# A spare PSUM bank as two halves in turn, in a planned attention and MLP kernel

## The chip, the cores and the metric

The kernel runs on one core of a Trainium2 chip. The metric is the device time of one execution in microseconds (us). "Span" is the time from the first to the last instruction of the profiled execution; it is about 1.8 us shorter than the device time of the same execution.

## The reference, cut to what matters

Two transformer layers with the same weights: layernorm, attention with 16 heads of 28 columns over 2048 tokens of 448 columns, then layernorm and an MLP of 1792 hidden columns with a squared ReLU.

```python
x = A_x
for layer in range(2):                      # the same weights twice
    h = layernorm(x)
    q, k, v = heads(h @ wqkv)               # 16 heads of 28
    p = softmax(q @ k.T * 28 ** -0.5)       # 16 x 2048 x 2048
    x = x + merge(p @ v) @ wo
    h = layernorm(x)
    x = x + relu(h @ w1 + b1) ** 2 @ w2 + b2
```

## The kernel before

The exponentials of the softmax are the largest single piece of work: 16 x 2048 x 2048 of them per layer, for both layers together done by ScalarE in 683 instructions ("exps" below) of 128 x 1536. Everything else is laid around them. A small planner inside the program does that before anything runs: each piece of work is an `Op` with an engine, an assumed duration, what it depends on and the buffer that it takes. The planner repeatedly issues the candidate that can start first by its own model. The order that comes out is fixed; on the chip each engine works its queue strictly in that order, and if the model was wrong, it stands.

```python
class Res:                                   # a buffer with n places
    def when(self):                          # when the next taker may have it
        k = len(self.rel)
        return 0.0 if k < self.n else self.rel[k - self.n]
...
    # in the planner: work of lower rank goes to TensorE only if it ends
    # no later than SLACK after the next exp's scores are due
    ok = [c for c in cands if c[2] != "PE" or c[1] == 0 or c[0] + c[3][2].dur <= due + SLACK]
    cands = ok or cands
```

The kernel uses eight PSUM banks. Six hold two score groups (three units of 512 columns each), one holds the value sums, and one spare bank takes everything else: projections, transposes, both MLP layers and the "fillers", matmuls without a use of their own that are meant to keep TensorE's clock up. (In the trace of this kernel the granted clock is 0.5 from 151.6 to 155.0 us, just after TensorE has stood for 3.06 us.) Emptying the spare bank into SBUF is called an eviction.

```python
R_sc, R_o, R_m, R_pt = Res(2), Res(1), Res(1), Res(4)
...
def bank(o, name):
    if o.res is R_m:
        return ps_m.tile([P, 512], DT.float32, name=name, tag="m")[:, :]
    return ps_sc.tile([P, 3 * 512], DT.float32, name="sc", tag="sc")[:, 0:512]
...
def mm_tile(subs, evac, ev_dur, deps, any_engine=False, sets=(), early=False):
    ...                                      # the matmuls of one tile into bank(first)
    e = Op(..., ev_dur, lambda e: evac(e, box["t"]), deps=[last], rel=first, sets=sets)
    yield e                                  # the eviction, in the same stream
    return e
```

A unit is one head's scores of one key block (128 keys) against 512 queries; three units make a group with one exp. `AHEAD = range(2)` tells how many of the four head groups of the second layer's second query block are begun before the last key blocks are needed. `SLACK = 0.7` is the microseconds by which lower work may overrun the time when the next scores are due.

```python
add_passes(1, [0], [0, 12])                  # layer 2, query block 0: keys 0..11
add_passes(1, [1], [0, 12], AHEAD)           # query block 1, some head groups: keys 0..11
add_passes(1, [0], [12, 16])                 # only now keys 12..15
```

The softmax denominators of most query blocks are spread over partitions through DRAM and broadcast back, by three queued transfers with assumed latencies:

```python
d1 = Op("DMA", 0.1, spread, deps=[oe])       # + 2.0 for any DMA
...
d2 = Op("DMA", 0.1, away, deps=[r1])
...
r = own = Op("DMA", 1.0, back, deps=[d2], acq=R_rec)
```

The softmax here doesn't subtract the row's maximum and nothing guards it: scores larger than these inputs give would overflow.

Of the kernel before, what the change touches and what calls it, by code (L numbers as in the profile page):

```python
# [23 lines left out]
AHEAD = range(2)  # L24
SLACK = 0.7
# [15 lines left out]
class Op:  # L41
    __slots__ = ("eng", "dur", "fn", "deps", "acq", "rel", "mode", "sets", "start", "end", "res", "turn", "ready")

    def __init__(self, eng, dur, fn, deps=(), acq=None, rel=None, mode="full", sets=()):
        self.eng = eng if isinstance(eng, tuple) else (eng,)
        self.dur, self.fn, self.deps, self.rel, self.mode = dur, fn, deps, rel, mode
        self.acq = acq if isinstance(acq, tuple) else (() if acq is None else (acq,))
        self.sets = sets if isinstance(sets, list) else ([sets] if sets else [])
        self.start = self.end = self.res = self.turn = None

# [4 lines left out]
class Planner:  # L55
# [3 lines left out]
    def __init__(self):  # L59
# [4 lines left out]
        self.past = []  # L64

# [5 lines left out]
    def spawn(self, prio, gen):  # L71
        self.streams.append([prio, gen, next(gen, None)])
        self.streams.sort(key=lambda s: s[0])

    def earliest(self, o):
        t = 0.0
        for d in o.deps:
# [5 lines left out]
            t = max(t, d.end + ((0.06 if same else 0.10) if d.eng[0] == "DVE" else  # L83
                                (0.0 if same and d.eng[0] != "DMA" else LAT[d.eng[0]])))
        if o.acq:
# [3 lines left out]
            t = max(t, min(free))  # L89
        o.ready = t  # L90
# [9 lines left out]
    def run(self):  # L100
        while self.streams:
# [20 lines left out]
            o.start, o.end = s, s + o.dur  # L122
            self.clock[e] = o.end
# [8 lines left out]
            st[2] = next(st[1], None)  # L132
# [5 lines left out]
def kernel(  # L138
# [40 lines left out]
    R_sc, R_o, R_m, R_pt = Res(2), Res(1), Res(1), Res(4)  # L179
    R_xt, R_os, R_xn, R_h, R_on, R_rec = Res(3), Res(2), Res(2), Res(1), Res(2), Res(2)  # L180
# [104 lines left out]
    def bank(o, name):  # L285

        if o.res is R_m:
            return ps_m.tile([P, 512], DT.float32, name=name, tag="m")[:, :]
# [11 lines left out]
    def layernorm(t0, nt, deps_of, early=False):  # L300
# [39 lines left out]
        def turn(p0, own, xs):  # L340
            def tr(e, xs=xs):
                tp = bank(t, "tp").bitcast(DT.bfloat16).rearrange("p (c q) -> p c q", c=NDC)
# [5 lines left out]
            t = Op("PE", 0.07 * NDC * len(xs), tr, deps=[x[1] for x in xs], acq=pools_now(early))  # L348
            yield t

            def ev(e, tp=box["t"], p0=p0, w=len(xs) * P):
# [6 lines left out]
            yield o  # L358
# [3 lines left out]
        for p0 in range(0, nt, 2):  # L362
            js = range(p0, min(p0 + 2, nt))
            own = Op("DVE", 0.0, None, acq=R_xn)
            yield own
            xs = []
            for j in js:
                xn = xns[2 * (own.turn % 2) + j % 2]
# [10 lines left out]
            if early and p0 + 2 < nt:  # L379
                continue  # L380
# [5 lines left out]
    def mm_tile(subs, evac, ev_dur, deps, any_engine=False, sets=(), early=False):  # L386
# [7 lines left out]
        while i < len(mms):  # L394
# [5 lines left out]
            def fn(e, part=mms[i:k], i=i):  # L400
                if i == 0:
                    box["t"] = bank(first, "mt")
                for c0, n, lhsT, rhs, a, b in part:
                    nc.tensor.matmul(box["t"][:, c0:c0 + n], lhsT=lhsT, rhs=rhs, start=a, stop=b)  # L404
            last = Op("PE", dur, fn, deps=list(deps) if i == 0 else [last],
                      acq=pools_now(early) if i == 0 else None)
# [3 lines left out]
        e = Op(engs_now(early) if any_engine else ("DVE",), ev_dur, lambda e: evac(e, box["t"]), deps=[last], rel=first, sets=sets)  # L410
        yield e
        return e

    def copy_to(dst):
        def f(e, t):
            src = t[:, :] if len(dst.shape) == 2 else t[:, :].rearrange("p (r n) -> p r n", r=dst.shape[1])
# [6 lines left out]
    def qkv(l, t0, nt, xnT, own_xt, ends, early=False):  # L423
        n, q0 = nt * P, t0 * P
        r = QB // n
        last = None

        def turned(w, dst, key, wkey, g0):
            nonlocal last
            d = dst[:, g0, q0:q0 + n] if r == 1 else dst[:, g0:g0 + r, q0:q0 + n]  # L430
            last = yield from mm_tile(
                [(i * n, n, [(w[:, dc, 4 * g:4 * g + 4, :], xnT[:, dc, 0:n]) for dc in range(NDC)])
                 for i, g in enumerate(range(g0, g0 + r))],
                copy_to(d), 0.70, [*ends, *[(wkey, g) for g in range(g0, g0 + r)]], True,
                [(key, l, g, tb) for g in range(g0, g0 + r) for tb in range(t0, t0 + nt)], early)

        def values():
            nonlocal last
            for tb in range(t0, t0 + nt):
                def evv(e, t, tb=tb):  # L440
                    o = V_sb[l][:, tb, :, 0:DH]
                    i = t[:, 0:D].rearrange("p (h r) -> p h r", r=DH)
                    if e == "ACT":
                        nc.scalar.copy(out=o, in_=i)
                    else:
                        nc.vector.tensor_copy(out=o, in_=i)  # L446
                j = tb - t0
                last = yield from mm_tile(
                    [(0, D, [(xnT[:, dc, j * P:(j + 1) * P], wv[:, dc, :]) for dc in range(NDC)])],
                    evv, 0.62, [*ends, ("wv",), *([("s", 1)] if early else [])], True, ("V", l, tb), early)  # L450

        ks = [(wk, K_sb[l], "K", "wk", g) for g in range(0, G, r)]
        qs = [(wq, Q_sb, "Q", "wq", g) for g in range(0, G, r)]
# [99 lines left out]
    def p_stream():  # L553
        for gi, us in enumerate(groups):
# [5 lines left out]
            for ri, run in enumerate(runs):  # L560
# [8 lines left out]
                def fn(e, gi=gi, us=us, run=run, box=box, opens=opens, l=l, g=g, kbs=kbs, r=r, n=n):  # L569
                    if opens:  # L570
                        box["t"] = ps_o.tile([P, QB], DT.float32, name="oT")
                    for i in range(r):
# [9 lines left out]
                       deps=[("e", gi), *{("V", l, us[k][1] + i) for k in run for i in range(r)}],  # L582
# [24 lines left out]
    def norm_stream(l, qb, g, res, oe):  # L607
# [6 lines left out]
        if tail:  # L614
            def den(e):
                box["t"] = bank(d, "den")
# [173 lines left out]
```

## Time and profile before

| kernel before | value | from |
|---|---|---|
| device time | 991.0 us median (987.35 to 991.94, 4 runs) | the runs beside the changed kernel |
| span, granted clock | 990.1 us, 0.990 | the profile by core |
| ScalarE / TensorE / VectorE busy | 937.5 / 913.4 / 419.5 us | the page, first part |
| first exp starts; tail after the last exp | 14.6; 31.5 us | the trace |
| typical distance of two exp starts | 1.33 us | the trace |
| gaps: all distances of exp starts, less 1.335 each | 32.4 us | the trace |
| of it short gaps (distance 1.375 to 2.6 us) | 25.8 us in 83 | the trace |
| of it long gaps (distance over 2.6 us) | 7.4 us in 2 | the trace |

This is one time budget: head, 682 distances of 1.335, gaps, last exp, tail. As long as the pace of 1.33 us stays, a change of the kernel shows in the head, the gaps and the tail and nowhere else. A gap that is named by its place ("after exp 351") is given as the whole distance of two exp starts. I use the split into short and long gaps. (Distances below 1.375 are in the total only, so the two kinds don't add up to it exactly.) The lines of the page and of the timeline are shown and read in the prediction. One more, of the groups by form: the eviction of the MLP's first layer, a whole bank, 691 ns each.

```profile
L701 DVE TENSOR_SCALAR r<-mt 128x512 bf16<-128x512 f32 x100 | 69.1, 691 | 89.6 <-PE mt L404 89.5
```

### The profile page before, as it was taken

To read this page: it belongs to the slowest core of one execution; us is meant where nothing else is said; L and a number is where in the kernel's file an instruction comes from. 1 tells how busy PE (TensorE), PEld (TensorE's weight loads), DVE (VectorE), ACT (ScalarE), POOL (GpSimd) and SP (SyncE) were. 2 spreads that over 40 slices of the span, in tenths; PEclk is the share of its full clock that TensorE was granted. 3 is DMA by queue.
4 is the path that set the end of the run, shared out by engine and by line. 5 is a ranking of instruction groups with operands and counts; after the bars stand their busy time and mean duration, and the time that the engine had idled before them with its cause. 6 is when DMAs were issued, how large, how long until landed. Compare 5 with 4: busy or idle time off the path is not lost.

```text
span 990.1 us, 15972 instructions
## 1 busy us (share of the span) xinstructions
PE 913.4 (92%) x6679; PEld 316.3 (32%) x6679; DVE 419.5 (42%) x935; ACT 937.5 (95%) x704; POOL 7.5 (1%) x16
## 2 busy tenths in 40 slices
PE   8899998999999999999999999888999998899988
PEld 3233322233233322333223333222333332333345
DVE  7744415524355144652445423225525510343264
ACT  5999998999999999999999999998999999999982
POOL 3000000000000000000000000000000000000000
PEclk9999999999999999999999999999999999999999
DMA  9000010000000000000000000010000000000000
GB/s 268 3 1 1 2 43 4 12 12 13 12 12 1 12 12 13 1 1 1 1 1 1 1 1 1 15 43 13 13 30 12 7 25 12 19 7 12 20 2 19
DMA packets 19732, 16.75 MB, mean 17 GB/s; under 512 B 8394, under 2 KB 16139, under 8 KB 19660
## 3 DMA queue, kind: packets, MB, share of 16 engines
q1 hardware_dynamic: 19660, 15.74, 5.2%
q8 instruction: 52, 0.85, 0.3%
q14 instruction: 20, 0.16, 0.1%
HBM read 13.47 MB, written 2.05 MB: 16 GB/s over the span
## 4 chain that ended last, share of the span: by engine, by line
ACT 45%; PE 19%; issue 17%; DMA 12%; DVE 7%; ACTq 0%; DVEq 0%; SPq 0%
ACT pt L545 45%; DMA rec<-scr 8%; PE mt L404 7%; PE sc L530 4%; PE oT L576 3%; DMA scr<-dn 3%; PE mt L744 2%; PE sc L404 2%; DMA dn<-oT_sb 1%; DVE oTn L661 1%; DVE r L701 1%; PE tp L346 1%; DVE xnT L356 1%; DVE x_sb L672 1%; DVE st L308 1%
## 5 line engine op out<-in xcount | busy, mean ns | idle before, releaser
L545 ACT ACTIVATE pt<-sc 128x1536 bf16<-128x1536 f32 (+1 forms) x683 | 923.2, 1517 | 21.3 <-PE sc L530 20.3
L530 PE MATMUL sc<-Q_sb,K_sb 32*128 32x512 bf16 (+1 forms) x2304 | 269.4, 361 | 33.6 <-ACT pt L545 26.5
L576 PE MATMUL oT<-pt,V_sb 128*32 128x512 bf16 (+1 forms) x2304 | 266.6, 366 | 4.2 <-DVE oT_sb L601 1.6
L530 PEld LDWEIGHTS <-K_sb 32*128 32x128 bf16 x2304 | 79.7, 91 | 277.2 <-issue 268.6
L576 PEld LDWEIGHTS <-V_sb 128*32 128x32 bf16 x2304 | 69.6, 93 | 157.2 <-issue 155.4
L404 PE MATMUL mt<-xnT,w 128*128 128x512 bf16 (+1 forms) x432 | 108.2, 371 | 6.5 <-DVE r L701 0.9
L701 DVE TENSOR_SCALAR r<-mt 128x512 bf16<-128x512 f32 x100 | 69.1, 691 | 89.6 <-PE mt L404 89.5
L672 DVE TENSOR_TENSOR x_sb<-x_sb,mt 128x448 bf16<-128x448 bf16 x60 | 37.2, 621 | 161.2 <-PE mt L404 161.2
L744 PE MATMUL mt<-xn,ident 128*128 128x448 bf16 x269 | 88.9, 361 | 12.1 <-DVE xn L371 3.0
L404 PE MATMUL mt<-w,h 128*128 128x448 bf16 x406 | 93.5, 354 | 1.9 <-DVE x_sb L672 1.2
L404 PEld LDWEIGHTS <-w 128*128 128x128 bf16 x504 | 43.7, 97 | 54.1 <-issue 27.2
L661 DVE TENSOR_TENSOR oTn<-oT_sb,rec 128x512 bf16<-128x512 f32 (+1 forms) x36 | 22.7, 630 | 70.7 <-DMA rec<-scr 70.5
L404 PEld LDWEIGHTS <-h 128*128 128x128 bf16 x448 | 36.9, 97 | 46.4 <-issue 23.0
L708 DVE TENSOR_TENSOR h<-r 128x512 bf16<-128x512 bf16 x112 | 47.3, 423 | 6.6 <-ACT r L699 3.6
L308 DVE BATCH_NORM_STATS2 st<-x_sb 128x6 f32<-128x448 bf16 x64 | 38.6, 602 | 0.8 <-DMA x_sb<-in_A_x_dram 0.8
L404 PE MATMUL mt<-wo,oTn 128*128 128x448 bf16 x124 | 31.4, 362 | 6.8 <-DVE oTn L661 4.5
L420 DVE CAST K_sb<-mt 128x512 bf16<-128x512 f32 x30 | 20.7, 690 | 35.0 <-PE mt L404 34.8
L446 DVE CAST V_sb<-mt 128x448 bf16<-128x448 f32 x31 | 19.3, 624 | 36.9 <-PE mt L404 36.9
L404 PE MATMUL mt<-xnT,wq 128*128 128x512 bf16 x124 | 32.5, 380 | 1.8
L404 PE MATMUL mt<-xnT,wk 128*128 128x512 bf16 x120 | 32.6, 388 | 1.5
L420 DVE CAST Q_sb<-mt 128x512 bf16<-128x512 f32 x30 | 20.7, 691 | 30.3 <-PE mt L404 30.3
L744 PEld LDWEIGHTS <-ident 128*128 128x128 bf16 x269 | 18.5, 97 | 43.0 <-issue 42.8
(74 smaller groups left out, 349.4 us busy)
## 6 DMA issues: line engine op xcount, KB each, us to landing
rec<-scr SPq DMA_DIRECT2D x24, 256.0 KB
x_sb<-in_A_x_dram SPq DMA_DIRECT2D x8, 224.0 KB
out_dram<-x_sb SPq DMA_DIRECT2D x16, 112.0 KB
w<-in_B_w_dram SPq DMA_DIRECT2D x1, 1568.0 KB
w<-in_B_w_dram SPq DMA_DIRECT2D x1, 1344.0 KB
part_sb<-in_A_wqkv_dram SPq DMA_DIRECT2D x1, 672.0 KB
rec<-scr SPq DMA_DIRECT2D x4, 128.0 KB
wo<-in_A_wo_dram SPq DMA_DIRECT2D x4, 98.0 KB
```

The source lines that it names most:

```text
L308: nc.vector.bn_stats(out=st[:, :], in_=x_sb[:, t0 + j, :])
L404: nc.tensor.matmul(box["t"][:, c0:c0 + n], lhsT=lhsT, rhs=rhs, start=a, stop=b)
L420: nc.vector.tensor_copy(out=dst, in_=src)
L446: nc.vector.tensor_copy(out=o, in_=i)
L530: nc.tensor.matmul(sc[:, c0:c0 + nt * P], lhsT=K_sb[l][rows, g, (kb + i) * P:(kb + i + 1) * P], rhs=Q_sb[rows, g, t0 * P:(t0 + nt) * P], s ...
L545: nc.scalar.activation(out=pt[:, 0:n], in_=gbuf[gi]["sc"][:, 0:n], func=AF.Exp, scale=scale)
L576: nc.tensor.matmul(box["t"][DHP * hh:DHP * hh + DHP, 0:n], lhsT=V_sb[l][:, kb + i, 4 * g + hh, :], rhs=gbuf[gi]["pt"][:, c0:c0 + n], start ...
L661: nc.vector.tensor_tensor(out=oTn_of[l, qb][0][:, g, 0:n], in0=res["t"][:, 0:n], in1=box["r"][:, 0:n], op=ALU.mult)
L672: nc.vector.tensor_tensor(out=x_sb[:, tb, :], in0=x_sb[:, tb, :], in1=t[:, 0:D], op=ALU.add)
L701: nc.vector.tensor_scalar(out=r[:, 0:w], in0=t[:, 0:w], scalar1=0.0, scalar2=None, op0=ALU.max)
L708: nc.vector.tensor_tensor(out=h[:, 0:w], in0=r[:, 0:w], in1=r[:, 0:w], op=ALU.mult)
L744: nc.tensor.matmul(t[:, 0:D], lhsT=ident[:, :], rhs=xns[0][:, 0:D], start=True, stop=True)
```

## The change

Its intent: in the kernel before, TensorE must wait with the next tile until VectorE has emptied the spare bank. With the bank as two halves of 256 columns, used in turn, one half would be filled while the other is emptied. Evictions become streams of their own, so that a tile's successor isn't ordered behind its eviction; the value matmuls of two score groups go together, to save TensorE's switches between kinds of matmul; and the plan gets longer latencies for the three DMA transfers. Two constants change along with it. The core of the diff (of about 500 lines):

```diff
-AHEAD = range(2)
-SLACK = 0.7
+AHEAD = range(1)
+SLACK = 0.6
+W = 256
+BACK = 2.8
...
-    R_sc, R_o, R_m, R_pt = Res(2), Res(1), Res(1), Res(4)
+    R_open = Res(1)
+    R_sc, R_o, R_m, R_pt = Res(2), Res(1), Res(2), Res(4)
...
+    halves = ps_m.tile([P, 2 * W], DT.float32, name="halves")
+
-    def bank(o, name):
+    def bank(o):
         if o.res is R_m:
-            return ps_m.tile([P, 512], DT.float32, name=name, tag="m")[:, :]
+            return halves[:, o.turn % 2 * W:o.turn % 2 * W + W]
...
-        yield e
+        def leave():
+            yield e
+            yield from then
+        pl.spawn(None, leave())
...
-                       deps=[("e", gi), *{("V", l, us[k][1] + i) for k in run for i in range(r)}],
+                       deps=[("e", min(gi | 1, len(groups) - 1)), *{("V", l, us[k][1] + i) for k in run for i in range(r)}],
...
-            d1 = Op("DMA", 0.1, spread, deps=[oe])
+            d1 = Op("DMA", 0.5, spread, deps=[oe], lat=0.8)
-            d2 = Op("DMA", 0.1, away, deps=[r1])
+            d2 = Op("DMA", 0.4, away, deps=[r1], lat=-0.2)
-            r = own = Op("DMA", 1.0, back, deps=[d2], acq=R_rec)
+            own = Op("DMA", 0.5, back, deps=[d2], acq=R_rec, lat=BACK)
```

Not shown: every tile of 512 or 448 columns in the QKV projections, the output projection, both MLP layers and the fillers is cut into two of 256 or 224 (the first K and Q stay whole), and transposes go one block at a time, those of the first block excepted. And the early K, Q and V tiles of the first block, which in the kernel before could also go to a free score bank, go through the spare bank alone after the first K and Q.

## The prediction

> **What bounds the kernel now.** I read the page's busy shares and slices first, then its chain of work and its groups, then the list of waits, then stretches of the timeline. From the page:
>
> ```profile
> PE 913.4 (92%) x6679; PEld 316.3 (32%) x6679; DVE 419.5 (42%) x935; ACT 937.5 (95%) x704; POOL 7.5 (1%) x16
> ACT  5999998999999999999999999998999999999982
> PEclk9999999999999999999999999999999999999999
> ACT pt L545 45%; DMA rec<-scr 8%; PE mt L404 7%; PE sc L530 4%; PE oT L576 3%; DMA scr<-dn 3%; PE mt L744 2%; PE sc L404 2%; DMA dn<-oT_sb 1%; DVE oTn L661 1%; DVE r L701 1%; PE tp L346 1%; DVE xnT L356 1%; DVE x_sb L672 1%; DVE st L308 1%
> L545 ACT ACTIVATE pt<-sc 128x1536 bf16<-128x1536 f32 (+1 forms) x683 | 923.2, 1517 | 21.3 <-PE sc L530 20.3
> L744 PE MATMUL mt<-xn,ident 128*128 128x448 bf16 x269 | 88.9, 361 | 12.1 <-DVE xn L371 3.0
> ```
>
> The 683 exponentials on ScalarE are the spine: ScalarE is busy in every slice but the first and the last, at 80% or more. Their records overlap (1517 ns of record for 923.2 / 683 = 1.352 us of busy time), so I took the differences of successive exp starts in the trace: nearly all lie between 1.32 and 1.35 us, typically 1.335. The first exp starts at 14.6 us, the last ends at 958.6, and 31.5 us of tail follow. So
>
> 14.6 + 682 x 1.335 (910.5) + gaps + last exp 1.2 = 958.6, which makes the gaps 32 us.
>
> TensorE's 92% is no proof that it is full: L744 is 269 filler matmuls that only keep the clock up. But TensorE is strictly in order, and the score matmuls (S, L530) of the next exp stand in its queue behind value matmuls (P, L576) and a "fill" of projection or MLP work. Whatever holds the fill holds the next exp. The waits:
>
> ```profile
> ACT pt L545 <- PE sc L530: 20.3, 29, 4.2
> DVE oTn L661 <- DMA rec<-scr: 70.5, 25, 6.6
> ```
>
> A repeated small gap, in the timeline:
>
> ```profile
> 180.12 0.39 PE L530 MATMUL sc<-Q_sb,K_sb 32*128 32x512 bf16 x1
> 180.43 0.40 PE L576 MATMUL oT<-pt,V_sb 128*32 128x512 bf16 x3
> 180.44 0.68 DVE L701 TENSOR_SCALAR r<-mt 128x512 bf16<-128x512 f32 x1
> 180.76 0.10 PEld L404 LDWEIGHTS <-w 128*128 128x128 bf16 x1 [0.23 <-issue]
> 181.18 1.02 PE L404 MATMUL mt<-xnT,w 128*128 128x512 bf16 x4 [0.35 <-DVE r L701]
> 182.13 0.39 PE L530 MATMUL sc<-Q_sb,K_sb 32*128 32x512 bf16 x3
> 184.44 1.45 ACT L545 ACTIVATE pt<-sc 128x1536 bf16<-128x1536 f32 x1 [0.35 <-PE sc L530]
> ```
>
> The fill's weights are loaded at 180.76, but its single spare bank is still being emptied until 181.12; it starts 0.06 us later. S to S takes 2.01 us instead of 1.6, and two slots later ScalarE is idle. And a large gap:
>
> ```profile
> 146.93 0.74 PE L404 MATMUL mt<-wo,oTn 128*128 128x448 bf16 x3
> 149.98 0.69 DVE L661 TENSOR_TENSOR oTn<-oT_sb,rec 128x512 bf16<-128x512 f32 x1 [6.44 <-DMA rec<-scr]
> 150.73 0.36 PE L404 MATMUL mt<-wo,oTn 128*128 128x448 bf16 x1 [3.06 <-DVE oTn L661]
> 151.53 1.45 ACT L545 ACTIVATE pt<-sc 128x1536 bf16<-128x1536 f32 x1 [2.65 <-PE sc L530]
> ```
>
> The recorded plan believed that the reciprocal would be back from DRAM earlier; VectorE stands 6.44 us at its queue's head, TensorE 3.06, ScalarE 2.65.
>
> I sorted the 32 us by the longest TensorE stall within each late exp's slot: about 11 us the spare bank's eviction (fills of QKV and MLP waiting for VectorE), 7.5 the output projection waiting for oTn, 4 the clock fillers (also waiting for the bank), 5 slots simply filled too full, 5 the first two gaps near 20 us (K, Q and V of block 0).
>
> **What the Trainium skill says.** "Perfetto Trace Analysis", section "Identifying Performance Opportunities", says that the same bubble repeated on the engine that should be saturated can mean too few buffers, and its section "Matmuls" that groups should rotate through banks so that evictions overlap; the first half agrees with 180.76 to 181.18. "TensorE: Matmul & The Clock Gate", "Back-to-back issue gap", gives N/2.4 + 2.5 ns warm: 109 ns for 256 columns, 96 for 224. The trace agrees for 256: sixteen such matmuls take 1.91 us in the tail, 109 ns from start to start. The page's slower figure for streams with weight loads is not seen here. "PSUM — Partial Sum Buffer", "PSUM bank collisions raise a hardware error", warns that TensorE writing and VectorE reading the same bank and quadrant at once corrupts data, even at disjoint columns, and does not stall. The halves of the changed kernel share one bank, so the result wants checking; I take no time for it. No run yet shows it.
>
> **The change, part by part.**
>
> (a) Half banks. Every eviction of 512 or 448 columns becomes two of 256 or 224. Matmul time per column stays (2 x 109 against 216 ns). VectorE: 512 columns took 691 ns and 256 took 420, so a pair costs 0.15 us more; for 448, from the same line, 2 x 386 against 621. About 300 tiles x 0.15 = 46 us more VectorE work, 420 to 466 us, 47% of the span: off the path if it does not bunch. In the densest MLP pattern that the changed order has (three fills of two halves, then a slot without), VectorE has 6 x 0.42 + 3 squares x 0.42 = 3.8 us in four exps = 5.3 us, so it keeps up. What it buys: the next fill writes the other half, free for half a us or more by then. Of the 11 us I expect 9.5 back, of the 4 of the fillers 3.3.
>
> (b) Evictions as streams, queue latencies of 3.3 + 2.3 + 5.3 us in the plan in place of 2.1 + 2.1 + 3.0. In the trace one round trip takes 8.6 to 10 us from the copy into oT_sb to rec landing (171.24 to 179.80, 117.03 to 127.05). The plan goes from too short to slightly long, so the output projection is placed after its data is there. Of 7.5 us I expect 6 back, and most of the 70.5 us in which VectorE stood for rec, which pays for (a).
>
> (c) Value matmuls in pairs. Switching between S, P and fill costs 0.10 us each (S to P 0.32 us from start to start, of which 0.213 is the 512 columns). Between the first and the last S the orders have 1810 switches before and 1582 after: 228 x 0.10 = 23 us less on TensorE. The fillers grow from 265 x 189 ns = 50 us to 630 x 109 = 69, so the sum of TensorE's work in this stretch is unchanged, 827 against 829 us, both well under the 912 that ScalarE needs. The room is used for packing: MLP patterns of 1.30, 1.87, 1.30, 0.90 us per slot, 5.37 for four exps of 5.34. Tight, but the slack is cut from 0.7 to 0.6. Of the 5 us of overfull slots I expect 1 back.
>
> (d) Head. TensorE's work between the fifth and sixth S falls from 6.0 to 4.5 us, and in the next slot from 1.66 to 0.22: 2 us back.
>
> (e) Tail. Before the last S the order now finishes nearly the whole first MLP layer of the last but one block: behind it stand 60 matmuls of 256 columns instead of 104, 4.8 us less. But the tail is a chain: last value matmuls, sum, reciprocal (1.76 us), output projection, norm (2.4), transposes, 56 x 109 = 6.1, 60 x 96 = 5.8, store 2.6. Now the last value group stands behind two half tiles of second-layer work (2 x 1.44 us) although its exp is over 2 us earlier, which delays the chain by about 2; in return the first layer starts without the 1.6 us wait behind the other block's second layer that it has now (copy done 973.24, matmul 974.87). I make it 30.8 us instead of 31.5.
>
> Sum of gaps back: 9.5 + 3.3 + 6 + 1 + 2 = 21.8; tail 0.7. Estimate: 991.4 - 22.5 = 969, and I add 1 for stalls of a kind not listed: **970 us**.
>
> **Rivals.** 1. VectorE becomes the wait: twice the evictions, all in order behind reductions and adds. For it: 0.15 us more per tile and bursts of four halves. Against it: 47% share, and 70 us of standing taken away. It would leave 10 us more gaps: 980. 2. TensorE is truly full at ScalarE's real pace, since the plan reckons 1.372 us per exp and the trace shows 1.335: 251 pairs of neighbouring slots exceed 2.67 us after, 158 before. Those waits were partly hidden in the bank's wait before. It would give 976. 3. Everything fits, gaps fall to the head's 3 us: 962. 4. The clock falls with lighter fillers: TensorE's matmuls then last longer (0.61 for 0.39 us after the stall at 151 shows it); with 630 fillers I give it little.
>
> **Range and chances.** 962 to 982 covers rivals 1 to 3. A gain over 2% needs less than 971.6 us, 1.6 above my number: 0.57 faster, 0.41 within, 0.02 slower.
>
> **What would show it.** Exp starts still 1.335 us apart, first exp at 14.6, gap total about 11 us, tail near 31; the wait of ScalarE for S under 9 us from 20.3; VectorE busy near 466 us and its wait for rec well under 30 us; fills following P after 0.32 us. Wrong if VectorE leads the TensorE stalls, if exps come at over 1.35 us throughout MLP stretches, or if the tail grows past 33 us.

## The result, and the profile after

The changed kernel takes **1030.24 us** (1028.9 to 1030.42, 4 runs) against 991.0 (987.35 to 991.94, 4 runs): ratio 1.04, 95% interval 1.0372 to 1.0428, so slower by 4%. Its output is correct. (Here and below a ratio is the mean time of one kernel's fast runs over that of the other's of the same rounds, so it isn't quite the ratio of the medians.) The mean granted clock is 0.990 in both profiles, 20.5 us at half clock in each, so as a whole the clock isn't it. Where these stretches lie matters for the head and the tail, as is told below.

| | before | changed |
|---|---|---|
| span | 990.1 | 1028.5 |
| first exp; typical distance | 14.6; 1.33 | 14.6; 1.33 |
| gaps | 32.4 | 67.7 |
| short gaps | 25.8 in 83 | 53.8 in 163 |
| long gaps | 7.4 | 13.5 |
| tail after the last exp | 31.5 | 34.6 |

The gaps grew by 35.3 us and the tail by 3.1; together that is the 38.4 us of the spans. From the page of the changed kernel, busy shares, chain and the exponentials' group:

```profile
PE 893.1 (87%) x8424; PEld 466.8 (45%) x8424; DVE 445.9 (43%) x1249; ACT 945.0 (92%) x707; POOL 7.5 (1%) x16
...
PE 49%; ACT 23%; issue 14%; DVE 13%; DMA 0%; ACTq 0%; DVEq 0%
...
L592 ACT ACTIVATE pt<-sc 128x1536 bf16<-128x1536 f32 (+1 forms) x683 | 932.9, 1501 | 46.8 <-PE sc L577 37.4
```

TensorE is busy for less time than before although it has more instructions. The busy shares of TensorE and ScalarE fall, VectorE's rises by one point to 43%; the kernel waits more. ScalarE's idle time before exps has more than doubled, and the chain, which ran on ScalarE for 45% of the span and through DMA for 12% before, now runs on TensorE for 49%, on ScalarE for 23% and on VectorE for 13%. From the list of waits of the changed kernel (us in all, times, longest):

```profile
DVE oTn L716 <- DMA rec<-scr: 56.4, 13, 6.7
...
ACT pt L592 <- PE sc L577: 37.4, 70, 8.7
...
PE halves L439 <- DVE r L765: 20.7, 47, 0.9
...
PE halves L439 <- DVE x_sb L728: 10.4, 29, 0.5
```

In the kernel before, TensorE waited for the first layer's eviction 0.9 us in all, 2 times, by the same list. (A stall of the weight load just before is counted elsewhere, so this list is a lower limit in both.) I sorted the gaps of the changed kernel as in the prediction, by the longest TensorE stall in each late exp's slot: the spare bank's eviction now has 44 us in 103 gaps, the head 8.8, slots too full 7.3, the output projection 2.8. (No view prints this sort; it is an estimate. A simpler rule, tried on the same trace, gives about 46 for the spare bank, 8.8 for the head and 10 for full slots.)

Here is how it looks in the timeline, in the first MLP layer:

```profile
202.93 1.05 PE L439 MATMUL halves<-xnT,w 128*128 128x256 bf16 x8
...
204.01 0.76 DVE L765 TENSOR_SCALAR r<-halves 128x256 bf16<-128x256 f32 x2 [0.95 <-PE halves L439]
...
204.82 1.03 PE L439 MATMUL halves<-xnT,w 128*128 128x256 bf16 x8
...
205.79 0.39 PE L577 MATMUL sc<-Q_sb,K_sb 32*128 32x512 bf16 x3
205.90 0.76 DVE L765 TENSOR_SCALAR r<-halves 128x256 bf16<-128x256 f32 x2 [0.66 <-PE halves L439]
...
206.70 1.03 PE L439 MATMUL halves<-xnT,w 128*128 128x256 bf16 x8 [0.52 <-DVE r L765]
...
207.67 0.39 PE L577 MATMUL sc<-Q_sb,K_sb 32*128 32x512 bf16 x3
...
208.17 2.79 ACT L592 ACTIVATE pt<-sc 128x1536 bf16<-128x1536 f32 x2 [0.43 <-PE sc L577]
```

Each row of 8 matmuls fills both halves, four matmuls each. If the halves were two buffers, VectorE could start on the first half about 0.4 us before the row ends, and TensorE could fill the first half again while the second is being emptied. Neither happens. Both evictions start after all eight matmuls, and the next fill starts at 206.70, 0.04 us after both evictions have ended (205.90 + 0.76 = 206.66). The idle time is put down to VectorE's eviction by a semaphore event, so it is a wait that the program sets. The semaphores of the instructions show how: of the eight matmuls only the eighth raises the one that both evictions wait for, and only the second eviction raises the one that the next fill waits for. So the waits cover both halves together, not the columns that are read. The score matmuls behind the fill then come late, and ScalarE stands for 0.43 us. I counted over the whole trace how often a matmul into the spare bank runs while VectorE reads it: **0 of 289 evictions by VectorE before (251 without transposes and sums), 0 of 590 in the changed kernel**. The pair of half evictions takes 0.76 us where the whole one took 0.69.

The head shows the same alternation at its barest. K and Q of the first block go through the bank one after the other:

```profile
24.14 1.80 PE L439 MATMUL halves<-xnT,wk 128*128 128x256 bf16 x8
...
25.98 0.75 DVE L461 CAST K_sb<-halves 128x256 bf16<-128x256 f32 x2 [2.01 <-PE halves L439]
26.79 1.03 PE L439 MATMUL halves<-xnT,wq 128*128 128x256 bf16 x8 [0.84 <-DVE K_sb L461]
```

TensorE stands for 0.84 us, the exp after this waits for 8.66 us, and the gap at 20 us is 10.14 us long where it was 5.68. Two other things are in it. The granted clock was 0.5 from 22.3 to 25.7 us, which shows in the 1.80 us of the first row against 1.03 of the third. And the kernel before put some of these early tiles into score banks; with the whole spare bank but the rest of the change (e15, e13) this gap is still 7.26 and 7.69 us.

### The profile page after: what moved, and what is told of

The parts are those of the page before. It is cut to its first block, busy times and chain, and to the rows that moved or that the text cites. A ratio compares the mean times of both kernels' runs of the same rounds, so it can differ in the third digit from the quotient of the medians.

```text
span 1028.5 us, 19789 instructions
## 1 busy us (share of the span) xinstructions
PE 893.1 (87%) x8424; PEld 466.8 (45%) x8424; DVE 445.9 (43%) x1249; ACT 945.0 (92%) x707; POOL 7.5 (1%) x16
## 4 chain that ended last, share of the span: by engine, by line
PE 49%; ACT 23%; issue 14%; DVE 13%; DMA 0%; ACTq 0%; DVEq 0%
PE halves L439 28%; ACT pt L592 23%; PE oT L623 9%; PE sc L577 9%; DVE r L765 3%; DVE rec L676 2%; DVE x_sb L728 1%; DVE K_sb L461 1%; PE sc L439 1%; PE halves L809 1%; DVE V_sb L491 1%; DVE Q_sb L461 1%; DVE st L335 1%; PE halves L670 1%; DVE xnT L388 1%
## 5 line engine op out<-in xcount | busy, mean ns | idle before, releaser
L592 ACT ACTIVATE pt<-sc 128x1536 bf16<-128x1536 f32 (+1 forms) x683 | 932.9, 1501 | 46.8 <-PE sc L577 37.4
L623 PE MATMUL oT<-pt,V_sb 128*32 128x512 bf16 (+1 forms) x2304 | 211.2, 363 | 1.3 <-DVE part_sb L646 0.6
L439 PE MATMUL halves<-xnT,w 128*128 128x256 bf16 x868 | 115.8, 274 | 21.9 <-DVE r L765 20.6
L728 DVE TENSOR_TENSOR x_sb<-x_sb,halves 128x224 bf16<-128x224 bf16 x122 | 44.9, 386 | 189.8 <-PE halves L439 176.2
L765 DVE TENSOR_SCALAR r<-halves 128x256 bf16<-128x256 f32 x210 | 80.4, 419 | 85.7 <-PE halves L439 82.8
L439 PEld LDWEIGHTS <-w 128*128 128x128 bf16 x896 | 84.4, 99 | 61.5 <-issue 51.7
L809 PE MATMUL halves<-xn,ident 128*128 128x256 bf16 x630 | 107.0, 276 | 3.7 <-DVE ve L345 1.5
L439 PE MATMUL halves<-w,h 128*128 128x224 bf16 x840 | 100.0, 262 | 8.4 <-DVE x_sb L728 6.3
L439 PEld LDWEIGHTS <-h 128*128 128x128 bf16 x896 | 80.5, 98 | 32.9 <-issue 31.2
L754 DVE TENSOR_TENSOR h<-r 128x512 bf16<-128x512 bf16 (+1 forms) x126 | 49.0, 392 | 10.0 <-ACT r L763 7.7
L716 DVE TENSOR_TENSOR oTn<-oT_sb,rec 128x512 bf16<-128x512 f32 (+1 forms) x36 | 22.5, 624 | 56.4 <-DMA rec<-scr 56.4
L439 PE MATMUL halves<-xnT,wk 128*128 128x256 bf16 x248 | 34.7, 276 | 7.7 <-DVE K_sb L461 4.9
L461 DVE CAST Q_sb<-halves 128x256 bf16<-128x256 f32 x62 | 24.1, 420 | 31.5 <-PE halves L439 31.3
```

Source lines behind the costliest of these rows:

```text
L439: nc.tensor.matmul(box["t"][:, c0:c0 + n], lhsT=lhsT, rhs=rhs, start=a, stop=b)
L461: nc.vector.tensor_copy(out=dst, in_=src)
L592: nc.scalar.activation(out=pt[:, 0:n], in_=gbuf[gi]["sc"][:, 0:n], func=AF.Exp, scale=scale)
L623: nc.tensor.matmul(box["t"][DHP * hh:DHP * hh + DHP, 0:n], lhsT=V_sb[l][:, kb + i, 4 * g + hh, :], rhs=gbuf[gi]["pt"][:, c0:c0 + n], start ...
L716: nc.vector.tensor_tensor(out=oTn_of[l, qb][0][:, g, 0:n], in0=res["t"][:, 0:n], in1=box["r"][:, 0:n], op=ALU.mult)
L728: nc.vector.tensor_tensor(out=xs, in0=xs, in1=t[:, 0:D // 2], op=ALU.add)
```

## The experiments

**Theory A**, formed from these traces: the halves of one bank never overlap, by the waits that the program gets, while the plan believes that they do (`Res(2)`); so it lays fills where TensorE must stand. The rivals: the pairs of value matmuls (they delay the value sums and fill slots unevenly), and the rest of the change (streams, latencies, the two constants). The texts say what each expects. All kernels gave correct results.

One table for all of them; "halves" or "whole" is the spare bank, "before" in the first column marks the kernel before as the basis. Ratios are to the kernel before in the same rounds. The sets ran on different chips, on which the kernel before had medians of 988.3 to 993.3 us, so differences of medians between sets are good to some 5 us. The sets were e1 to e4, e5 to e7, e8 to e11, e12 and e13, e14 to e16, and e17; e8 to e11 and e14 to e16 ran on the same chip.

| run | bank | pairs | ahead | slack | median us | ratio, 95% interval | short gaps | long gaps |
|---|---|---|---|---|---|---|---|---|
| before | whole | no | 2 | 0.7 | 991.0 | 1 | 25.8 | 7.4 |
| changed | halves | yes | 1 | 0.6 | 1030.2 | 1.04 (1.0372 to 1.0428) | 53.8 | 13.5 |
| e1 | whole | yes | 1 | 0.6 | 1024.2 | 1.0334 (1.0281 to 1.0387) | 8.9 | 53.8 |
| e2 | halves | no | 1 | 0.6 | 1016.5 | 1.0263 (1.0211 to 1.0315) | 37.4 | 11.2 |
| e3 before + pairs | whole | yes | 2 | 0.7 | 993.2 | 1.0029 (0.9976 to 1.0082) | 16.8 | 20.9 |
| e4 before + latencies | whole | no | 2 | 0.7 | 975.7 | 0.9865 (0.9797 to 0.9933) | 12.2 | 4.3 |
| e5, e6 (groups of two units) | halves in one, in two banks | yes | 1 | 0.6 | low clock, see text | none | | |
| e7 (plan: one place) | halves | yes | 1 | 0.6 | 1058.0 | 1.0704 (1.066 to 1.0747) | 12.4 | 77.9 |
| e8 | whole | yes | 2 | 0.6 | 1006.3 | 1.0171 (1.0134 to 1.0208) | 9.5 | 35.1 |
| e9 | halves | yes | 2 | 0.6 | 1026.0 | 1.0387 (1.035 to 1.0424) | 50.9 | 12.8 |
| e10 | whole | no | 2 | 0.6 | 990.6 | 1.0021 (0.9986 to 1.0056) | 10.3 | 22.4 |
| e11 before + latencies + pairs | whole | yes | 2 | 0.7 | 985.7 | 0.9963 (0.9924 to 1.0001) | 12.6 | 16.0 |
| e12 before + latencies + slack | whole | no | 2 | 0.6 | 995.9 | 1.0067 (1.0035 to 1.01) | 11.7 | 23.8 |
| e13 | whole | no | 2 | 0.7 | 977.4 | 0.9875 (0.9852 to 0.9898) | 11.8 | 8.0 |
| e14 | halves | yes | 1 | 0.7 | 1024.2 | 1.0353 (1.0311 to 1.0395) | 46.4 | 16.8 |
| e15 | whole | yes | 2 | 0.7 | 977.4 | 0.9884 (0.9852 to 0.9917) | 9.8 | 8.6 |
| e16 | halves | no | 2 | 0.7 | 1017.7 | 1.0297 (1.0258 to 1.0335) | 44.4 | 11.3 |
| e17 (plan: one place) | halves | yes | 2 | 0.7 | 1041.5 | 1.0492 (1.0469 to 1.0514) | 15.0 | 59.0 |

### First four: halves, pairs, latencies, each alone

**e1**: the changed kernel with a whole bank, tiles uncut.

```diff
-W = 256
+W = 512
-    R_sc, R_o, R_m, R_pt = Res(2), Res(1), Res(2), Res(4)
+    R_sc, R_o, R_m, R_pt = Res(2), Res(1), Res(1), Res(4)
...
-            return halves[:, o.turn % 2 * W:o.turn % 2 * W + W]
+            return whole[:, :]
... (and every loop over half tiles back to one tile, transposes by two blocks)
```

> The changed kernel with the two half banks undone alone: one spare bank of 512 columns with one user at a time, tiles of 512 or 448 columns again; evictions as streams, paired value matmuls, DMA latencies, the changed slack and order of passes are kept. Theory A (the halves never overlap: an eviction of one half waits for the matmuls of the other, and the reverse, while the plan believes that they do): 975 to 995 us, the exp gaps back to 35 us or less from 67. Rival B (the paired value matmuls, which put six in a row before the next scores): still above 1015. Rival C (VectorE overloaded by twice the evictions) expects the same as A here.

Measured 1024.15 us. Theory A's number failed by 30 us. But the kind of gap changed: short gaps fell from 53.8 to 8.9 us, as theory A has it, and two single gaps of 19.0 and 19.9 us appeared, after exps 351 and 420, that the changed kernel doesn't have. That fits that the halves made the short gaps, and something else was hidden behind them.

**e2**: the changed kernel without pairs.

```diff
-                       deps=[("e", min(gi | 1, len(groups) - 1)), *{("V", l, us[k][1] + i) ...
+                       deps=[("e", gi), *{("V", l, us[k][1] + i) ...
```

> The changed kernel with the pairing undone alone: each value group waits for its own exp again. Theory A: still slow, 1015 to 1040 us, since the halves are still there. Rival B: under 1005.

Measured 1016.47 us, 14 less than the changed kernel, still 2.6% slower than before. Pairs matter here, and aren't the main part.

**e3**: the reverse edit in the kernel before, pairs alone.

> The kernel before with the pairing added alone. Theory A: 978 to 995 us, no harm, perhaps some gain from fewer switches. Rival B: above 1005.

Measured 993.24 us, no difference that the interval allows to name.

**e4**: the kernel before with nothing but the DMA latencies (the lines of d1, d2 and `back` in the diff above, and the field `lat`).

> The kernel before with the DMA latencies of the changed plan added alone. If the prediction's part (b) was right, the stalls of the output projection for the reciprocal (7.5 us of exp gaps) fall to 2 or less and the time to 983 to 988 us; if the planned order gives it back elsewhere, 989 to 993.

Measured 975.66 us, ratio 0.9865, better than expected and **faster than both kernels** (the interval, 0.9797 to 0.9933, lies below 1). From its list of waits, to be set against the two lines in the prediction (20.3 and 70.5 us):

```profile
DVE oTn L662 <- DMA rec<-scr: 35.3, 9, 8.3
...
ACT pt L546 <- PE sc L531: 6.3, 7, 4.2
```

All gaps together are 15.9 us instead of 32.4. Sorted as in the prediction, those of the output projection fell from 7.5 to 0.9 us, and with them the others, the spare bank's from 9.1 (the prediction has about 11 for this kind; the sort is no more exact than that) to 6.5, the fillers' from 4.2 to 1.4, overfull slots' from 5.2 to 2.7. That fits, but isn't shown by a run of its own, a VectorE that stands less at its queue's head and does its other evictions in time. One of the four runs took 981 us, the other three 974 to 977, which makes the interval wide.

### The mechanism of the halves: e5, e6, e7

All eight banks are in use (6 + 1 + 1), so there is none for a second spare. With score groups of two units instead of three, two banks come free, so that the same order of instructions can be run with the two halves in one bank (e5) and in two (e6).

```diff
-        return ps_sc.tile([P, 3 * 512], ...
+        return ps_sc.tile([P, 2 * 512], ...
-    groups = [units[i:i + 3] for i in range(0, len(units), 3)]
+    groups = [units[i:i + 2] for i in range(0, len(units), 2)]
... e6 only:
-    halves = ps_m.tile([P, 2 * W], DT.float32, name="halves")
+    halves = [ps_m.tile([P, W], DT.float32, name=f"half{i}", tag=f"half{i}") for i in range(2)]
```

> The changed kernel with score groups of two units in place of three (exps of 1024 columns), which frees two PSUM banks; the two halves still share one bank. A control for the next run, slower than the changed kernel or near it for its 1024 shorter exps: 1040 to 1120 us under every theory.

> The same with the second half in a bank of its own; the order of instructions on every engine is identical to the run before (compared row by row), only where the second half lies and so which waits the framework sets differ. Theory A: at least 25 us faster than the run before, the evictions start 0.1 us after the fourth matmul of their own half, and TensorE's waits for VectorE fall to a third or less. Rival C (VectorE overloaded by twice the evictions) or D (TensorE too full): within 8 us of the run before.

As times both are inconclusive: every run had a low mean clock (1117 to 1325 us at 0.885 to 0.697, and 1123 to 1194 us at 0.871 to 0.792). The fastest of each kernel, 1117.15 and 1123.24 us, are within the 8 us of rivals C and D, at unequal clocks. What made the clock fall stays open. As a look at the mechanism the runs are not inconclusive: a matmul into the spare space began during an eviction from it in **0 of 588** evictions in e5 and in **241 of 588** in e6. The same eight matmuls and two evictions, both at full clock, in e5 and in e6:

```profile
163.65 0.94 PE L439 MATMUL halves<-wo,oTn 128*128 128x224 bf16 x8
...
164.63 0.69 DVE L728 TENSOR_TENSOR x_sb<-x_sb,halves 128x224 bf16<-128x224 bf16 x2 [1.45 <-PE halves L439]
```

```profile
206.20 0.94 PE L439 MATMUL half<-wo,oTn 128*128 128x224 bf16 x8
206.79 0.77 DVE L728 TENSOR_TENSOR x_sb<-x_sb,half 128x224 bf16<-128x224 bf16 x2 [1.29 <-PE half L439]
```

In e6 the eviction of the first half begins at 206.79, when the second half's matmuls run until 207.14; the fourth matmul raises a semaphore of its own. In e5 both evictions wait for the eighth. So where the second half lies decides. The second half of e6 is another bank and also another tile of the framework; which of the two makes the wait, no run separates.

The traces also tell roughly what two banks are worth. TensorE's waits for VectorE in the lists of waits fell from 30.9 us in 49 to 12.2 us in 16, to 40% where I expected a third. And in the 71 of 127 stretches of eight exps in which both kernels had a granted clock over 0.995, e5 took 552.1 us and e6 541.7, 1.9% less with the same order of instructions. For groups of three units it stays open.

**e7**: the changed kernel, with the plan told the truth, one place instead of two.

```diff
-    R_sc, R_o, R_m, R_pt = Res(2), Res(1), Res(2), Res(4)
+    R_sc, R_o, R_m, R_pt = Res(2), Res(1), Res(1), Res(4)
```

> The changed kernel with half tiles as they are, but the plan told that there is one spare turn: a tile may start only when the one before has been evicted. Theory A (the harm is that the plan counts on an overlap that the chip's waits forbid, so that matmuls are queued ahead of scores while their bank is not free): exp gaps fall to under 45 us from 67, time 985 to 1015 us, though the evictions stay as small and as many. Rival C (many small evictions): no better than 1025.

Measured 1057.97 us, slower still, against the expectation. Short gaps fell to 12.4 us, but all gaps together are 89.2 us, not under 45: gaps of 30.6 and 24.5 us stand after the same exps 351 and 420 as in e1. Two kernels with two long gaps in the same places asked for a reason.

### The hidden deadline: e8 to e13

What is at exp 351? The first layer has 1024 units. The second begins with 48 units of one head group over key blocks 0 to 11, so unit 1024 + 32 = 1056 is the first that needs key block 8. With three units per group that is group 1056 / 3 = 352, whose exp follows exp 351. Key blocks 8 to 11 are the third query block of layer 1: it must have passed its output projection, MLP, layernorm and key projection by then. And key block 12 is first needed at unit 1024 + 192 + 48 = 1264, group 421, with `AHEAD = range(1)`, and at unit 1024 + 192 + 96 = 1312, group 437, with `range(2)`. The long gap after exp 420 is this second deadline, which the changed constant sets 16 exps, 21 us, earlier.

**e8** and **e9** are e1 and the changed kernel with that constant back; **e10** is e8 without pairs.

```diff
-AHEAD = range(1)
+AHEAD = range(2)
```

> The whole-bank kernel (first experiment) with two head groups worked ahead over the layer boundary again, as before, in place of one. That experiment lost about 37 us in two long gaps of ScalarE, 19 and 20 us, near exps 351 and 420. If those come from the shorter stretch of work ahead (theory E): they are gone, and the time is 970 to 990 us, which also restores theory A for the rest (spare-bank stalls 12 us there against 44 in the changed kernel). If the two gaps stay, the change of order is not their cause: above 1010.

> The changed kernel with two head groups ahead, all else kept. Its trace has no such long gap at the boundary, so theory A expects little: 1018 to 1034 us. If the order of passes were what makes the changed kernel slow: under 1005.

> The whole bank, two head groups ahead and no pairing: what remains of the change is evictions as streams, the DMA latencies and the smaller slack. Theory A with the latencies as the only useful part: 970 to 982 us, like the kernel before with the latencies alone (975.7).

e8 took 1006.34 us, between its two expectations: the gap after exp 420 is gone (18 us less than e1), the one of 19.0 us after exp 351 stays. e9 took 1026.0 us, only 4 less than the changed kernel. At this point halves cost 20 us against e8's whole bank. e10 took 990.56 us, and missed its expectation (970 to 982): gaps of 4.3 to 7.7 us remain, at exps 351, 436 and 441 among others, and it has none of e4's gain.

**e11**: e4 with pairs.

> The kernel before with the DMA latencies and the pairing. If the pairing is neutral where the spare bank is whole (993 against 991 alone): 972 to 979 us. If it costs by itself what its removal gave in the changed kernel (14 us): 985 to 993.

985.67 us, 10 more than e4. Its short gaps are e4's (12.6 against 12.2 us); most of the difference is gaps of 4.75, 3.6 and 4.46 us after exps 351, 436 and 441, and there are two of about 3 us elsewhere (exps 237 and 327). So pairs cost mostly at the layer's boundary.

**e12** and **e13** split the 15 us between e4 and e10. The slack is the only constant left: e12 is e4 with slack 0.6, e13 is e10 with slack 0.7.

```diff
 e12:                e13:
-SLACK = 0.7        -SLACK = 0.6
+SLACK = 0.6        +SLACK = 0.7
```

> The kernel before with the DMA latencies (975.7 us) and, in addition, the changed kernel's slack of 0.6 instead of 0.7. The whole-bank version of the changed kernel without pairs and with two groups ahead took 990.6 although it has the same latencies; 15 us between the two belong to the slack, to the evictions as streams of their own, or to the smaller things left (unpacked tiles of the two-block query blocks, transposes). Theory slack: 985 to 992 here. Theory streams and rest: 973 to 979.

> The other way round: whole bank, two groups ahead, no pairs, streams kept (990.6 us), slack back to 0.7. Theory slack: 974 to 981. Theory streams and rest: 987 to 993.

995.93 us and 977.41 us: the first 4 us beyond theory slack's range, the second inside it. The slack alone adds 20 us to e4 and takes 13 from e10. In e12 it is one gap, of 20.8 us after exp 351 (e4 has none there), and the trace shows it to be the deadline:

```profile
493.63 1.69 PE L405 MATMUL mt<-w,h 128*128 128x448 bf16 x8
...
496.22 0.92 PE L405 MATMUL mt<-wo,oTn 128*128 128x448 bf16 x4 [0.17 <-DVE x_sb L673]
...
512.93 0.69 DVE L421 CAST K_sb<-mt 128x512 bf16<-128x512 f32 x1 [0.48 <-PE mt L405]
...
513.68 1.04 PE L531 MATMUL sc<-Q_sb,K_sb 32*128 32x512 bf16 x6 [0.79 <-DVE K_sb L421]
...
514.39 1.45 ACT L546 ACTIVATE pt<-sc 128x1536 bf16<-128x1536 f32 x1 [19.32 <-PE sc L531]
```

After exp 351 TensorE has nothing but the late block's own chain, the MLP's end, layernorm and keys, and between these the next block's output projection, four tiles through the same spare bank (the first at 496.22). The scores start at 513.68, when VectorE has written K. With 0.1 us less slack per slot less of this work fitted between exps earlier on: when exp 351 starts, TensorE has done 695 matmuls of projections, MLP and sums in e4 and 638 in e12. What was missing came here all at once.

Not all of the gap is lateness. The granted clock was 0.5 for 14.0 of its 20.8 us (from 500.4 us on). TensorE was busy for 7.9 of these 14, so some 4 us are lost to the clock, an estimate. The long gaps of the other kernels hold such stretches too: after exp 351, 12.0 of 19.0 us in e1 and e8, 10.7 of 28.5 in e17.

### The parts by themselves, with the deadline out of the way: e14 to e17

**e14**: the changed kernel with `SLACK = 0.7`. **e15**: e8 with 0.7. **e16**: e13 with half banks and what belongs to them (all half tiles, transposes by one block and `Res(2)` as in the changed kernel).

> The changed kernel (1030 us) with the slack back to 0.7, everything else kept. The changed kernel has no long gap at the layer's boundary (exp 351), its gaps are short ones at the spare bank. Theory A, the slack costs time only by the boundary's deadline and the halves' waits make the rest: 1020 to 1032, spare-bank gaps still above 35 us. Rival, the slack itself costs 13 to 20 us in any version: 1008 to 1018.

> Whole bank, two groups ahead, pairs kept (1006 us with slack 0.6, of which one gap of 19 us stands at exp 351, where the keys of block 2 of the second layer are due), slack 0.7. Deadline theory: that gap goes, 984 to 991, and the pairs' cost against the version without them (977.4 us) is then 7 to 13. Rival, pairs alone make the boundary late: the gap stays, 1000 or more.

> The version of 977.4 us (whole bank, two ahead, no pairs, slack 0.7) with nothing but half banks in place of the whole one. Theory A (the halves of one bank never overlap and their handover costs): 992 to 1008, no eviction overlapped by a matmul into the bank, spare-bank gaps of 20 us or more. Rival (halves as such are harmless, other parts did the damage): 974 to 985.

e14: 1024.17 us, as theory A had it. The changed kernel has no long gap at the boundary, and its slack costs it only 6 us, 5 by the ratios, which is about the spread between sets. e15: 977.35 us, better than expected. It holds all of the change but the half banks and the two constants, with pairs, and is as fast as e13 without them: pairs cost and gain nothing once the deadline is met. e16: 1017.72 us. **Half banks alone cost 40.3 us** (1017.72 - 977.41; e13 ran on another chip, and by the ratios it is 42), more than theory A's number. The spans differ by 39.1 us: gaps 56.1 against 19.1, the rest head and tail. It is the short gaps that grow, from 11.8 us in 67 to 44.4 us in 173. From the lists of waits, e13 first:

```profile
ACT pt L592 <- PE sc L577: 10.3, 6, 6.2
...
PE whole L439 <- DVE rec L676: 1.7, 3, 1.0
```

```profile
ACT pt L592 <- PE sc L577: 31.6, 63, 6.5
...
PE halves L439 <- DVE r L765: 13.0, 62, 0.8
```

In e13 the largest such wait of a fill is 1.7 us in all, and none for the MLP's first layer is listed (stalls under 0.15 us are not); in e16 the eviction of the MLP's first layer leads with 62 stalls, and ScalarE waits for scores 63 times instead of 6.

**e17**: is the loss only the plan's false belief? e7 once more, with both constants back.

```diff
 (the changed kernel with)
-AHEAD = range(1)
-SLACK = 0.6
+AHEAD = range(2)
+SLACK = 0.7
-    R_sc, R_o, R_m, R_pt = Res(2), Res(1), Res(2), Res(4)
+    R_sc, R_o, R_m, R_pt = Res(2), Res(1), Res(1), Res(4)
```

> Half banks kept, but the plan told that they are one place (as in e7), with two groups ahead and slack 0.7 so that the second layer's deadline is not missed. Theory, the halves lose because the plan believes in an overlap that never comes: short gaps at the spare bank fall to about 12 us as in e7, no gap over 10 us, time 978 to 992, near the whole bank's 977. Rival, half tiles lose in themselves, since each handover to VectorE and back is paid twice: long gaps at the boundary stay or TensorE fills up, 1000 or more.

1041.46 us: my theory missed, the rival's "1000 or more" holds. The short gaps did fall, to 15.0 us, but the gap at the boundary is 28.5 us long and the tail longer by 8 than e15's. So the half tiles lose in themselves, and telling the plan the truth doesn't mend it. At the boundary, where no other work hides anything, the cost can be read off, at a granted clock of 1.0 in both stretches. First e17, half tiles of the MLP's second layer, then e8, a whole tile of the same:

```profile
515.07 1.50 PE L439 MATMUL halves<-w,h 128*128 128x224 bf16 x14 [0.48 <-DVE x_sb L728]
...
517.15 1.50 PE L439 MATMUL halves<-w,h 128*128 128x224 bf16 x14 [0.48 <-DVE x_sb L728]
```

```profile
500.40 2.82 PE L439 MATMUL whole<-w,h 128*128 128x448 bf16 x14
...
503.05 0.35 PE L439 MATMUL whole<-b2w,one 128*128 128x448 bf16 x1
...
503.44 0.62 DVE L728 TENSOR_TENSOR x_sb<-x_sb,whole 128x448 bf16<-128x448 bf16 x1 [2.37 <-PE whole L439]
...
504.12 0.92 PE L439 MATMUL whole<-wo,oTn 128*128 128x448 bf16 x4 [0.17 <-DVE x_sb L728]
```

A half tile takes 517.15 - 515.07 = 2.08 us from start to start, two of them 4.16; a whole tile takes 504.12 - 500.40 = 3.72. The matmul time is the same; the second handover to VectorE and back, with the longer evictions (2 x 0.39 against 0.62), costs 0.44 us. With the true plan the loss shows as lateness at the deadline and in the tail, with the false one as short stalls everywhere. Either way it is there. How much of the 40 us is the second handover and how much the plan's false belief, these runs don't divide.

## Why the prediction was wrong

Predicted 970 us, range 962 to 982, with a chance of 0.02 for slower; measured 1030.

- **The step that failed is part (a)**: "the next fill writes the other half, free for half a us or more by then. Of the 11 us I expect 9.5 back, of the 4 of the fillers 3.3." I had it in front of me, in "The halves of the changed kernel share one bank, so the result wants checking; I take no time for it." I took the collision as a question of right results. But a program that is right in spite of it must have a wait there, and that wait makes the two halves one buffer whose tile is handed over twice. The runs showed 0 of 590 evictions overlapped, spare-bank gaps of 44 us instead of about 1.5, and 40 us for the half banks alone (e16 against e13), of which the short gaps make 33. No rival of mine had the wait that stays; rival 1, VectorE as the bound, has the right engine and the wrong reason: VectorE's busy time is 445.9 us, 26 more and not the 46 that I reckoned, as a pair of evictions took 0.76 us and not 2 x 0.42.
- **(b) Latencies**: the mechanism was right and the term too small. Alone they brought 15 us (e4) where I expected 6 plus what VectorE's freed time would pay. In the changed kernel the output projection's gaps fell from 7.5 to 2.8 us (I had 1.5), VectorE's wait for the reciprocal from 70.5 to 56.4 us only, not to under 30. (The plan's second latency is 0.4 + 2.0 - 0.2 = 2.2 us, not the 2.3 of the prediction.) I haven't tested the streams by themselves; e15, which has them, is no faster than e4.
- **(c) Pairs**: I expected 1 us back. With the deadline met they make no difference (e15 and e13); in the changed kernel undoing them gains 14 us (e2). "Of the 5 us of overfull slots I expect 1 back" became 7.3 us of such gaps. "The room is used for packing" and "the slack is cut from 0.7 to 0.6" stood there as a remark, and `AHEAD` not at all. Beside a whole bank these two constants are worth 13 to 29 us (e13 to e10, e15 to e8) and 18 us (e8 to e1), by a deadline at the layer's boundary that I never looked for. In the changed kernel they are worth 6 and 4 (e14, e9), hardly more than the spread between sets.
- **(d) Head**: predicted 2 us back, measured 3.9 more (8.8 against 4.9). It is the same alternation of fill and eviction, which I counted as TensorE's work only, and not of the halves alone: the early tiles no longer had the score banks, and the clock was 0.5 in a part of it.
- **(e) Tail**: predicted 30.8 us, measured 34.6. I had no stall of the clock in it. TensorE stands 4.98 us for the last layernorm (until 1008.10), and the granted clock is 0.5 from 1005.3 to 1015.5 us; in the tail before it is 1.0 throughout. TensorE is busy for 6.66 us in that stretch, which at full clock would be about 3.3 us less, an estimate, as much as the growth. All seven kernels with half banks and groups of three units have 6.8 to 10.2 us at half clock in their tails, none with a whole bank more than 1.2. Why the stall there is longer, no run tests.
- **Right**: first exp at 14.6 us, pace 1.33 us, the mean clock unchanged, VectorE not full, and what I named as the sign of failure, "Wrong if VectorE leads the TensorE stalls" and "if the tail grows past 33 us"; both happened.

How the 53 us between e15 or e13 (977.4) and the changed kernel divide: 40 are the half banks, measured with all else of the program equal. The other 13 are slack, groups ahead and pairs on top of half banks; undone singly they give 6, 4 and 14, so they don't simply add. What stays open: why pairs cost 14 us beside half banks and slack 0.6, where nothing stands at the deadline, and what two real spare banks would bring to this kernel. One caution holds for every number here: the planner is greedy, so one constant changes the whole order, and a cost "of the slack" is the difference of two orders, not a law.

## What to carry to other kernels

Two halves of a bank are not two buffers when one wait covers both; before you count on an overlap, ask which wait lets it happen, and count in the trace whether a single one does. Cutting a tile for an overlap that doesn't come pays the handover twice. In a planned kernel, put latencies into the plan that are no shorter than the measured ones first (that alone gave 975.7 us, 1.3% under the kernel before, and no version was faster beyond the noise), list the deadlines that the order of data sets, and treat a constant that moves them as a change of its own. And look at the clock of a stretch, not only at its mean: a long stall can be followed by a slow stretch that is longer than itself (4.98 us and 10.2 us in the tail here).

## What the Trainium skill lacked or had wrong

- "PSUM — Partial Sum Buffer", section "PSUM bank collisions raise a hardware error", tells to guard by bank and speaks of errors and wrong data. It lacks the cost in time: with halves of one bank a matmul began during 0 of 590 evictions, with two banks during 241 of 588, and half tiles in one bank cost 40 us of 977.
- "Perfetto Trace Analysis", section "Matmuls", says to rotate through different banks. It doesn't warn that cutting one bank in two is no rotation, nor that each handover has its price: 0.44 us per tile of 448 columns when cut in two, where nothing else hid it.
- "TensorEngine Tiling (Array Packing)", section "Key Properties", says that a change of tiling mode drains TensorE, without a figure. Here a score group's last matmul to the first value matmul is 0.315 us from start to start (the median), while matmuls of 512 columns of one kind follow each other in 0.216: about 0.10 us per switch.
- "DMA: Bandwidth & Descriptors", section "Anatomy of one DMA — SWDGE (gpsimd) path", gives about 2 us of fixed cost and bytes over 436 GB/s for that path. SyncE's queue, used here, isn't in that fit: its three transfers in a row took 1.85, 1.40 and 4.99 us from issue to landing (the round trip that starts at 171.24), the last a 256 KB broadcast read for which that fit would give an estimate of 2.6 us.
- No page has the planning lesson: three DMA latencies in the model, together 3.6 us shorter than in the changed plan (2.1 + 2.1 + 3.0 against 3.3 + 2.2 + 5.3), were worth 15 us of 991.
